# Second norms of a token mixer: row sums carried by the passes instead of statistics instructions, and rows gated in another order

## The chip, the cores and the metric

The kernel runs on one core of one Trainium2 chip. A core has engines that work beside each other, each with its own queue in a fixed order: TensorE (PE) for matrix products, VectorE (DVE) and ScalarE (ACT) for passes over the elements of a tile, GpSimd (POOL) likewise but slower, and SyncE (SP), which here issues the DMAs. They hand over by semaphores. The metric is the time of one execution on the device in microseconds (us), as the median of several runs; smaller is better.

## The reference

A block of a sequence mixer on 2048 tokens with 640 channels, fp32. The layers' modulations `sa, ca, ga, sb, cb, gb` come from `silu(c) @ w_mod`.

```python
h = layernorm(x) * (1 + ca) + sa
x = x + ga * h3(h, k, v, ...)          # short and long causal convolutions, gated by h
h = layernorm(x) * (1 + cb) + sb       # h is then normalized once more inside B:
x = x + gb * B(h)                      # B: w2 . gelu(w1 . layernorm(h) + b1) + b2, over the tokens
```

What counts here is the middle: the x that leaves the first half is normalized over its 640 channels (first norm), scaled by 1 + cb and shifted by sb, normalized again (second norm), and then multiplied by w1, a product over the tokens.

## The kernel before, in words

The 2048 tokens lie as 16 tiles ("rows" j = 0 to 15) of 128 partitions by 640 channels, XR(j), rows 0 to 7 in one buffer (`xa`) and 8 to 15 in another (`xb`). The first half (lines 500 to 628) computes the long convolution as matrix products, in five chunks of 128 channels. At the end of a chunk, i1(half) (L266) leaves the convolution's result for eight rows in PSUM, gate (L293) multiplies it by A1 and adds it to x, both for eight rows at once, and spill (L300) writes x to DRAM by SP. Chunk 4 is the last one. Its second half is gated in the next stage.

The norm stage (lines 631 to 712) follows. Every engine's order is the order of the source: nothing is rescheduled. Its helpers are:

- mod_row (L353): PE spreads a row of the modulations over the partitions, ACT copies it: row 4 is CB = 1 + cb, row 3 is SB = sb, row 5 is GB.
- x1_stats (L642): on DVE, a statistics instruction for the last 128 channels of a row and one that aggregates those of the five chunks: mean and variance of the first norm.
- rstd (L307) and rstd_pool (L320): one over the root of the variance, by ACT's root, DVE's reciprocal and a step of refinement, on DVE or on POOL, where it is a chain of small instructions ("links"). rstd_pool also makes the negated mean times that.
- norm1 (L647): ACT writes the normalized row into a temporary `tmp`, of which there are six.
- mod_stats (L651): DVE multiplies by CB, adds SB, takes two statistics of 320 channels and aggregates them.
- norm2 (L661): ACT normalizes the temporary in place and writes its upper half, rounded to fp32r, as H[j][0].
- rests (L670): DVE subtracts; the low half goes to H[j][1].
- products (L674): PE multiplies rows 2 pr and 2 pr + 1 by the first four of 14 blocks of w1. A row and a block are six products (upper by upper, upper by low, low by upper, for two halves of 320 channels, L423 in mm), so a row feeds 24, and the four blocks' results stay in the four PSUM places.

The pairs of rows pass this as a pipeline, pr = 0 to 7. After it PE runs blocks 4 to 13, then the second matrix w2. load_w(i) (L389) issues a block's load, split_w(i) (L403) splits it into upper and low halves on ACT and DVE.

psum() (L69) gives out three PSUM places in turn, and four once the norm stage has begun. The line L59 is that of the helper TT, so all tensor_tensor instructions have it.

Of the kernel before, what the change touches and what calls it, by code (L numbers as in the profile page):

```python
# [49 lines left out]
def mixer_kernel(ctx: ExitStack, tc: tile.TileContext, q, k, v, shift_k, ssm_k, ssm_D, w1, b1, w2, b2, c,  # L50
# [8 lines left out]
    TT = lambda eng, o, a, b, op: eng.tensor_tensor(o, a, b, op=op)  # L59
# [7 lines left out]
    ring = [3]  # L67

    def psum():  # L69

        uid[0] += 1
        return psp.tile([128, 1024], F32, name=f"pst_{uid[0]}", tag=f"pst{uid[0] % ring[0]}", bufs=1)

    def dram(t, offset, ap):
        return bass.AP(tensor=t.tensor, offset=t.offset + offset, ap=ap)
# [6 lines left out]
    T_g, T_rows, T_t, sm = mem("g", 1280), mem("rows", 640), mem("t", 1280), mem("sm", 704)  # L82
# [23 lines left out]

    def small(n):
        so[0] += n
        assert so[0] <= 704
        return sm[:, so[0] - n:so[0]]  # L110

    cols = small(36)
# [3 lines left out]
    rs1, nm1, rs2, nm2, tm = small(16), small(16), small(16), small(16), small(16)  # L116
    ones = small(64)
    msk = small(1)
    epsc = small(1)
    B1C, B2C = cols[:, 0:14], cols[:, 14:30]  # L120

# [144 lines left out]
    def i1(half):  # L266

        ps = psum()
        for jj in range(8):
            for ri in range(2):  # L270
                for e in range(2):
                    p = slice(64 * e, 64 * e + 64)
                    for b in range(2):
                        n2 = 16 * b + 8 * half + jj
                        pe.matmul(ps[64 * b:64 * b + 64, 512 * e + 64 * jj:512 * e + 64 * jj + 64],  # L275
                                  V1[p, ri, n2], T2[p, :, 32 * ri + n2], start=ri == 0, stop=ri == 1)
        return ps
# [12 lines left out]
            ac, po = [lambda j=j: both(j) for j in range(16)], []  # L290
        return ac, po

    def gate(c, ps, half, eng=pool):  # L293
        a = A1[:, 8 * half:8 * half + 8]
        av = a.rearrange("p j (m e) -> p e j m", e=2)
        TT(dve, av, ps.rearrange("p (e j m) -> p e j m", e=2, j=8), av, ALU.mult)
        x = XH[half][:, :, DC * c:DC * c + DC]
        TT(eng, x, x, a, ALU.add)

    def spill(c):  # L300
        for half in range(2):
# [51 lines left out]
    def mod_row(i, t):  # L353

        ps, j = psum().rearrange("p (h m) -> p h m", h=2), i % 3
        for h in range(2):
            pe.matmul(ps[:, h, 0:320], ones[32 * j:32 * j + 1, 0:1].to_broadcast([1, 128]),
                      t[32 * j:32 * j + 1, 320 * h:320 * h + 320], start=True, stop=True)
        ps = ps[:, :, 0:320]
        two = lambda t: t.rearrange("p (h m) -> p h m", h=2)  # L360
        if i == 0:
            act.activation(two(G0), ps, AF.Copy)
        elif i == 1:
            act.activation(two(G1), ps, AF.Copy, bias=1.0)
        elif i == 2:
            TT(dve, two(G0), ps, two(G0), ALU.mult)
            TT(dve, two(G1), ps, two(G1), ALU.mult)
        elif i == 3:
            act.activation(two(SB), ps, AF.Copy)
        elif i == 4:  # L370
            act.activation(two(CB), ps, AF.Copy, bias=1.0)
        else:
            act.activation(two(GB), ps, AF.Copy)
# [15 lines left out]
    def load_w(i, t=X):  # L389
        if i >= NF + NW:  # L390
            return
        if i < NF:
            t = j16(t)
            for b in range(2):
                sync.dma_start(t[64 * b:64 * b + 64],
                               dram(w1, 16 * b * F + fo(i), [[32 * F, 64], [F, 16], [1, 128]]))
            raw[i] = (t, [slice(0, 8), slice(8, 16)])
        else:
            t = f14(t)
            load_w2(t, i - NF, 0, 14)  # L400
            raw[i] = (t, [slice(0, 7), slice(7, 14)])
# [98 lines left out]
    for c in range(NC):  # L500
# [91 lines left out]
        if cn is None:  # L592
            for kk in range(3, 5):
                mod_part(tap, kk, pl[kk])
            split_w(3, mem("y", 4096, "wb3"))
            load_w(4)
            mod_sum(tap, T_t[:, 0:640])
        if cn is not None:
            if c:
# [1 line left out]
            if c + 2 < NC:  # L601
                load_ks(c + 2)
        for half in range(2):
            ps = i1(half)
# [33 lines left out]
    ring[0] = 4  # L638
    uid[0] = 3
    acc = []  # L640

    def x1_stats(js):  # L642
        for j in js:
            x1s(NC - 1, j)()
            dve.bn_aggr(mv[:, j, :], bst[:, j])

    def norm1(pr):  # L647
        for j in (2 * pr, 2 * pr + 1):
            act.activation(tmp[j % 6], XR(j), AF.Identity, scale=rs1[:, j:j + 1], bias=nm1[:, j:j + 1])

    def mod_stats(js):  # L651

        for j in js:
            t = tmp[j % 6]
            TT(dve, t, t, CB, ALU.mult)
            TT(dve, t, t, SB, ALU.add)
            for h in range(2):
                dve.bn_stats(bst[:, j, h, :], t[:, 320 * h:320 * h + 320])
            dve.bn_aggr(mv[:, j, :], bst[:, j, 0:2, :])

    def norm2(pr):  # L661
        for j in (2 * pr, 2 * pr + 1):
            t = tmp[j % 6]
# [4 lines left out]
            act.activation(H[j][0].bitcast(F32R), t, AF.Copy)  # L668

    def rests(js):  # L670
        for j in js:
            TT(dve, H[j][1].bitcast(F32R), tmp[j % 6], H[j][0], ALU.subtract)

    def products(pr):  # L674
        if not acc:
            acc.extend(psum().rearrange("p (h m) -> p h m", h=2) for _ in range(4))
        js = [(f_, j) for j in (2 * pr, 2 * pr + 1) for f_ in range(4)]
# [3 lines left out]
    x1_stats(range(2))  # L681
    rstd(rs1, nm1, 0, 2)
    norm1(0)
    gate(NC - 1, ps, 1)
    spill(NC - 1)
    x1_stats(range(2, 8))
    rstd_pool(rs1, nm1, 2, 6, lambda: mod_stats([0]))
    mod_stats([1])
    norm1(1)
    rstd(rs2, nm2, 0, 2)  # L690
    mod_row(5, T_t[:, 0:640])
    norm2(0)
    for pr in range(1, 8):
        mod_stats([2 * pr])
        if pr == 1:
            rests([0])
        mod_stats([2 * pr + 1])
        if pr < 7:
            rstd_pool(rs2, nm2, 2 * pr, 2, lambda: rests([2 * pr - 1 if pr == 1 else 2 * pr - 2]))
            norm1(pr + 1)  # L700
            if pr == 1:
                x1_stats(range(8, 16))
                rstd_pool(rs1, nm1, 8, 8)
            else:
                rests([2 * pr - 1])
        else:
            rests((12, 13))
            rstd(rs2, nm2, 14, 2)
        norm2(pr)
        products(pr - 1)  # L710
    rests((14, 15))
    products(7)


# [11 lines left out]
    def u_evac(f, ps):  # L726
# [3 lines left out]
        for h in range(2):  # L730
# [8 lines left out]

    m_p = mem("p", 2048, "m_p")  # L740
    TU = [[(H[j][n][:, 0:320], H[j][n][:, 320:640]) for j in js for n in range(2)]
          for js in ((0, 1), (2, 3), (4, 5), (9, 10), (11, 12), (13, 14))]
    RB = thirds(m_p, 3, 1088)

    def t_ops(i):
# [237 lines left out]
```

## Time and profile before

| what | value |
|---|---|
| median of 3 runs | 759.33 us (758.6 to 759.56) |
| the profiled execution's own time | 755.42 us |
| its span in the profile | 753.6 us |
| granted TensorE clock, mean | 0.964 |
| busy: PE, DVE, ACT, POOL | 651.3, 507.3, 291.7, 162.7 us |

Times inside the trace count from the start of the span. A row of the view in order of time says when a group of instructions began, how long it took in all, its engine, its line, its operation, tiles and shape, how many there were, and in brackets how long the engine had been idle and who ended that. A row of the view of groups says busy time, the mean of one in ns, and the idle time before. A row of the stretches has busy time and number for PE, PE's weight loads, DVE, ACT and POOL, then the granted clock, the DMA share and GB/s. The page's digits are busy tenths of 40 equal slices.

### The profile page before, as it was taken

The numbers are of one execution on the slowest core, as the hardware profiler recorded it, in microseconds if no ns is written. First come the engines' busy times: TensorE is split into PE (matmuls) and PEld (weight loads), VectorE is DVE, ScalarE is ACT, GpSimd is POOL, SyncE is SP. The second block draws the span as 40 slices with busy tenths as digits, with TensorE's granted clock in tenths as the row PEclk, the third lists the DMA queues.
The fourth block names the chain that finished last, engine by engine and source line by source line (L and its number), as shares of the span: only waits on it lengthen the run. The fifth ranks groups of instructions, "written<-read, shape, count | busy, mean of one in ns | idle before, by whom it ended". The sixth has DMA issues, their size and how long they took to land.

```text
span 753.6 us, 20751 instructions
## 1 busy us (share of the span) xinstructions
PE 651.3 (86%) x9117; PEld 625.8 (83%) x9117; DVE 507.3 (67%) x889; ACT 291.7 (39%) x424; POOL 162.7 (22%) x167
## 2 busy tenths in 40 slices
PE   0598947698998988971799999999999989999997
PEld 0498737697898978850799999999999988999997
DVE  4667659975977936958998413113178959888887
ACT  0342324444553544544476523123134312332322
POOL 2359003802904805503452000000000000000000
PEclk9999979989999999975899999999999999999999
DMA  9998886218142036574000352533443252555420
GB/s 163 256 230 246 244 219 139 67 38 167 39 80 59 3 60 216 151 139 100 1 1 1 59 110 57 100 69 57 105 131 103 85 166 97 151 168 167 119 77 35
DMA packets 172425, 84.26 MB, mean 112 GB/s; under 512 B 88959, under 2 KB 164910, under 8 KB 172334
## 3 DMA queue, kind: packets, MB, share of 16 engines
q1 hardware_dynamic: 168110, 81.88, 44.2%
q10 hardware_dynamic: 4224, 1.05, 0.9%
q8 instruction: 71, 1.16, 0.7%
q14 instruction: 20, 0.16, 0.1%
HBM read 72.43 MB, written 10.49 MB: 110 GB/s over the span
## 4 chain that ended last, share of the span: by engine, by line
PE 53%; DVE 22%; POOL 7%; issue 5%; DMA 5%; ACT 5%; SPq 2%; ACTq 0%; DVEq 0%; POOLq 0%
PE pst L423 25%; PE pst L214 8%; PE pst L924 7%; POOL y L59 5%; PE pst L230 5%; DVE m_w L59 4%; PE pst L259 3%; PE pst L275 3%; DVE m_x L59 3%; ACT m_w L837 2%; DVE sm L525 2%; PE pst L849 2%; DVE tap L59 1%; DMA p<-in_B_w_dram 1%; DVE m_v L59 1%
## 5 line engine op out<-in xcount | busy, mean ns | idle before, releaser
L230 PE MATMUL pst<-z,w 128*64 128x64 f32 x2560 | 96.1, 240 | 7.6 <-ACT z L216 6.1
L230 PEld LDWEIGHTS pst<-z,w 128*64 128x64 f32 x2560 | 94.6, 141 | 9.5 <-ACT z L216 7.3
L59 POOL TENSOR_TENSOR y<-p 128x256 f32<-128x256 f32 x72 | 91.1, 1311 | 31.2 <-DVE p L59 30.9
L423 PE MATMUL pst<-r_z,wb 128*128 128x320 f32 x504 | 82.1, 319 | 16.1 <-ACT r_z L668 10.9
L423 PEld LDWEIGHTS pst<-r_z,wb 128*128 128x128 f32 x504 | 78.3, 196 | 18.0 <-ACT r_z L668 12.1
L216 ACT ACTIVATE z<-pst 128x1024 f32<-128x1024 f32 x40 | 45.7, 1142 | 68.8 <-PE pst L214 48.0
L59 DVE TENSOR_TENSOR p<-pst,kt 128x512 f32<-128x512 f32 x80 | 52.9, 690 | 27.0 <-ACT kt L234 18.6
L214 PEld LDWEIGHTS pst<-v,x 128*64 128x64 f32 x640 | 46.5, 222 | 6.6 <-POOL y L59 3.0
L214 PE MATMUL pst<-v,x 128*64 128x128 f32 x640 | 48.1, 317 | 4.1 <-DVE x L59 4.1
L423 PE MATMUL pst<-h_x,wb 128*128 128x320 f32 x336 | 51.1, 309 | 0.0
L423 PEld LDWEIGHTS pst<-h_x,wb 128*128 128x128 f32 x336 | 49.7, 188 | 0.0
L234 ACT ACTIVATE kt<-pst 128x512 f32<-128x512 f32 x40 | 25.2, 629 | 55.2 <-PE pst L230 27.2
L849 PE MATMUL pst<-r_z,m_w 128*128 128x320 f32 x222 | 43.1, 313 | 3.0 <-DVE m_w L59 2.5
L259 PEld LDWEIGHTS pst<-v,y 32*128 32x128 f32 x1280 | 39.5, 193 | 6.1 <-issue 3.4
L59 DVE TENSOR_TENSOR wb<-x,wb 128x1024 fp32r<-128x1024 f32 (+1 forms) x32 | 36.8, 1189 | 10.8 <-ACT wb L412 10.7
L259 PE MATMUL pst<-v,y 32*128 32x64 f32 x1280 | 41.2, 278 | 3.3 <-issue 2.0
L729 ACT ACTIVATE pst<-pst,sm 128x640 f32<-128x640 f32 x14 | 10.7, 766 | 86.0 <-PE pst L423 86.0
L214 PE MATMUL pst<-v,p 128*64 128x128 f32 x640 | 36.9, 274 | 3.6 <-ACT p L161 2.2
L275 PEld LDWEIGHTS pst<-z,v 64*64 64x64 f32 x1280 | 21.4, 140 | 21.7 <-issue 16.8
L849 PEld LDWEIGHTS pst<-r_z,m_w 128*128 128x128 f32 x222 | 34.8, 188 | 5.0 <-DVE m_w L59 4.1
L423 PE MATMUL pst<-h_a,wb 128*128 128x320 f32 x252 | 38.8, 309 | 0.0
L423 PE MATMUL pst<-r_v,wb 128*128 128x320 f32 x252 | 38.8, 309 | 0.0
(209 smaller groups left out, 1258.3 us busy)
## 6 DMA issues: line engine op xcount, KB each, us to landing
x<-in_B_w_dram SPq DMA_DIRECT2D x24, 512.0 KB
m_v<-in_B_w_dram SPq DMA_DIRECT2D x15, 384.0 KB
x<-in_B_w_dram SPq DMA_DIRECT2D x14, 384.0 KB
in<-in_A_k_dram SPq DMA_DIRECT2D x40, 128.0 KB
aux<-in_A_ssm_k_dram SPq DMA_DIRECT2D x10, 512.0 KB
m_x<-xs SPq DMA_DIRECT2D x28, 160.0 KB
out_dram<-m_x SPq DMA_DIRECT2D x28, 160.0 KB
w<-in_const_w_dram SPq DMA_DIRECT2D x2, 2048.0 KB
```

The lines of the kernel that those rows point to most:

```text
L59: TT = lambda eng, o, a, b, op: eng.tensor_tensor(o, a, b, op=op)
L214: pe.matmul(ps[64 * ri:64 * ri + 64, o:o + 128], lhs, F1[:, 128 * ri:128 * ri + 128], start=True, stop=True)
L216: evac = lambda: act.activation(Z[:, side, t].rearrange("p a k e -> p e a k"), ps.rearrange("p (e a k) -> p e a k", a=8, e=2), AF.Copy)
L230: pe.matmul(ps[64 * h:64 * h + 64, o:o + 64], W2[k1 // 32][:, 2 * (k1 % 32) + ri], rhs, start=True, stop=True)
L234: act.activation(kt.rearrange("p (m i) -> p m i", i=32), pv[:, :, 1], AF.Copy)
L259: pe.matmul(pp[qd // 2][:, o:o + 64], Y[p, ri, i:i + 2].rearrange("p i k -> p (i k)"), V2[p, 64 * ri:64 * ri + 64], start=ri == 0, stop=ri ...
L275: pe.matmul(ps[64 * b:64 * b + 64, 512 * e + 64 * jj:512 * e + 64 * jj + 64], V1[p, ri, n2], T2[p, :, 32 * ri + n2], start=ri == 0, stop=r ...
L423: pe.matmul(ps[0:m, h, 0:320], w_.bitcast(F32R), r_[:, 320 * h:320 * h + 320].bitcast(F32R), start=first and i == 0, stop=last and i == 2)
L525: dve.bn_stats(bst[:, j, h, :], XR(j, 320 * h, 320))
L837: act.activation(W[n][0].bitcast(F32R), a(w_), AF.Copy)
L849: pe.matmul(bank[n], w[:, i].bitcast(F32R), r.bitcast(F32R), start=i == 0 and k == 0, stop=i == 6 and k == 2)
L924: pe.matmul(acc[s][:, h, 0:320], w[:, f_].bitcast(F32R), u[r + h].bitcast(F32R), start=f_ == 0 and k == 0, stop=f_ == NF - 1 and k == 2)
```

## The change

The second norm no longer takes statistics. scaled(pr) multiplies a row by CB with scalar_tensor_tensor, which also gives the row's sum. centred(pr) makes minus the mean out of it and the sum of SB (which ACT's copy of SB now carries, `msb`) and adds that and SB in one pass. ACT squares the centred row, carrying the sum of squares (the squares themselves go to the place of the low half and are not used), and takes the root. root(pr) refines on POOL. halves(pr) scales and rounds on ACT in one pass; rests(pr) makes the low half with scalar_tensor_tensor out of the unscaled row. So a row has three DVE passes and three ACT passes of 640, where it had three passes, two statistics and an aggregation on DVE and three passes on ACT.

Around it, rows 0 to 3 of the last chunk's first half are gated before the stage, rows 4 to 7 inside it; the gate of the second half (rows 8 to 15) moves behind the root of rows 4 to 7; the first products begin with three blocks, as the fourth PSUM place still holds that half; the order of pairs is written anew; there are eight temporaries, in X, P and `g`; row 5 of the modulations goes up; the spill is split by halves; and load_w(4) goes behind the products of pair 5. The new line numbers: scaled L659, centred L664 and L667, the squares L672 and their root L673, root L679 to L685, halves L688, rests L692, norm1 L653, x1_stats L502 and L649, the negated mean of SB L372.

```diff
-    def gate(c, ps, half, eng=pool):
-        a = A1[:, 8 * half:8 * half + 8]
+    def gate(c, ps, half, eng=pool, j0=0, j1=8):
+        a = A1[:, 8 * half + j0:8 * half + j1]
...
         elif i == 3:
-            act.activation(two(SB), ps, AF.Copy)
+            act.activation(two(SB), ps, AF.Copy, accum_out=msb)
+            dve.tensor_scalar(msb, msb, -1 / D, None, op0=ALU.mult)
...
-            load_w(4)
             mod_sum(tap, T_t[:, 0:640])
...
-                gate(c, ps, 0, dve)
+                gate(c, ps, 0, dve, 0, 4)
...
-    mod_row(4, T_t[:, 0:640])
-    mod_row(3, T_t[:, 0:640])
+    s0, s1, s2 = ((uid[0] + i) % 3 for i in (-1, 0, 1))
+    mod_row(4, T_t[:, 0:640], s2)
+    mod_row(3, T_t[:, 0:640], 3)
+    mod_row(5, T_t[:, 0:640], s2)
...
-    H = (unit(r_z[:, 0:4096], 3) + unit(mem("aux", 4096, "h_a"), 3) + unit(r_v, 3)
+    H = (unit(r_z[:, 0:4096], 3) + unit(r_v, 3) + unit(mem("aux", 4096, "h_a"), 3)
          + unit(r_z[:, 3840:7680], 3))
-    tmp = piece(mem("p", 2048, "t_p"), 2) + piece(mem("g", 1280, "t_g"), 2) + piece(T_t, 2)
+    tmp = piece(X, 3) + piece(mem("p", 2048, "t_p"), 3) + piece(mem("g", 1280, "t_g"), 2)
...
-    def mod_stats(js):
-        for j in js:
-            t = tmp[j % 6]
-            TT(dve, t, t, CB, ALU.mult)
-            TT(dve, t, t, SB, ALU.add)
-            for h in range(2):
-                dve.bn_stats(bst[:, j, h, :], t[:, 320 * h:320 * h + 320])
-            dve.bn_aggr(mv[:, j, :], bst[:, j, 0:2, :])
...
+    def scaled(pr):
         for j in (2 * pr, 2 * pr + 1):
+            t = tmp[j % 8]
+            dve.scalar_tensor_tensor(t, t, 1.0, CB, op0=ALU.mult, op1=ALU.mult, accum_out=su[:, j:j + 1])
+
+    def centred(pr):
+        n = su[:, 2 * pr:2 * pr + 2]
+        dve.tensor_scalar(n, n, -1 / D, msb, op0=ALU.mult, op1=ALU.add)
+        for j in (2 * pr, 2 * pr + 1):
+            t = tmp[j % 8]
+            dve.scalar_tensor_tensor(t, t, su[:, j:j + 1], SB, op0=ALU.add, op1=ALU.add)
+        for j in (2 * pr, 2 * pr + 1):
...
-            act.activation(t, t, AF.Identity, scale=rs2[:, j:j + 1], bias=nm2[:, j:j + 1])
-            act.activation(H[j][0].bitcast(F32R), t, AF.Copy)
+            act.activation(H[j][1].bitcast(F32R), tmp[j % 8], AF.Square, accum_out=sq[:, j:j + 1])
+        act.activation(tm[:, 2 * pr:2 * pr + 2], sq[:, 2 * pr:2 * pr + 2], AF.Sqrt, scale=1 / D, bias=epsc)
+
+    def root(pr):
+        c2 = slice(2 * pr, 2 * pr + 2)
+        v_, r_, t_ = sq[:, c2], rs2[:, c2], tm[:, c2]
+        pool.tensor_scalar(v_, v_, 1 / D, EPS, op0=ALU.mult, op1=ALU.add)
+        dve.reciprocal(r_, t_)
+        TT(pool, t_, r_, r_, ALU.mult)
+        TT(pool, t_, t_, v_, ALU.mult)
+        pool.tensor_scalar(t_, t_, -0.5, 1.5, op0=ALU.mult, op1=ALU.add)
+        TT(pool, r_, r_, t_, ALU.mult)
+
+    def halves(pr):
+        for j in (2 * pr, 2 * pr + 1):
+            act.activation(H[j][0].bitcast(F32R), tmp[j % 8], AF.Identity, scale=rs2[:, j:j + 1])
...
+    x1_stats(range(4))
+    rstd(rs1, nm1, 0, 4)
     norm1(0)
...
     norm1(1)
+    gate(NC - 1, ps0, 0, dve, 4)
+    spill(NC - 1, (0,))
+    scaled(0)
+    centred(0)
+    scaled(1)
+    root(0)
+    centred(1)
+    halves(0)
+    x1_stats(range(4, 8))
+    root(1)
+    rests(0)
+    products(0, range(3))
+    rstd_pool(rs1, nm1, 4, 4, lambda: gate(NC - 1, ps, 1))
+    products(0, [3])
+    halves(1)
+    spill(NC - 1, (1,))
+    norm1(2)
+    rests(1)
+    products(1)
+    scaled(2)
+    centred(2)
+    norm1(3)
+    x1_stats(range(8, 16))
+    for pr in range(2, 8):
...
+            scaled(pr + 1)
+        root(pr)
+        if pr == 2:
+            rstd_pool(rs1, nm1, 8, 8)
+        if pr < 6:
+            norm1(pr + 2)
+        if pr < 7:
+            centred(pr + 1)
+        halves(pr)
+        if pr > 2:
+            rests(pr - 1)
+            products(pr - 1)
+        if pr == 6:
+            load_w(4)
+    rests(7)
     products(7)
```

The loop over the pairs before had, per pair, mod_stats of both rows, rstd_pool of the second norm, norm1 of the next pair, rests, norm2, and products of the pair before.

More of the change, by code (lines that the diff above doesn't have):

```diff
@@ L66, in mixer_kernel, with psum @@
     xs = drp.tile([S, D], F32, name="xs")
-    ring = [3]
-    def psum():
+    ring = [0, 1, 2]
+    def psum(slot=None):
         uid[0] += 1
-        return psp.tile([128, 1024], F32, name=f"pst_{uid[0]}", tag=f"pst{uid[0] % ring[0]}", bufs=1)
+        slot = ring[uid[0] % len(ring)] if slot is None else slot
+        return psp.tile([128, 1024], F32, name=f"pst_{uid[0]}", tag=f"pst{slot}", bufs=1)
     def dram(t, offset, ap):
@@ L118, in mixer_kernel @@
     msk = small(1)
+    su, sq, msb = small(16), small(16), small(1)
     epsc = small(1)
@@ L291, in a1_ops, with spill @@
         return ac, po
-    def gate(c, ps, half, eng=pool):
-        a = A1[:, 8 * half:8 * half + 8]
+    def gate(c, ps, half, eng=pool, j0=0, j1=8):
+        a = A1[:, 8 * half + j0:8 * half + j1]
         av = a.rearrange("p j (m e) -> p e j m", e=2)
-        TT(dve, av, ps.rearrange("p (e j m) -> p e j m", e=2, j=8), av, ALU.mult)
-        x = XH[half][:, :, DC * c:DC * c + DC]
+        TT(dve, av, ps.rearrange("p (e j m) -> p e j m", e=2, j=8)[:, :, j0:j1], av, ALU.mult)
+        x = XH[half][:, j0:j1, DC * c:DC * c + DC]
         TT(eng, x, x, a, ALU.add)
-    def spill(c):
-        for half in range(2):
+    def spill(c, halves=range(2)):
+        for half in halves:
             for b in range(2):
@@ L603, in mixer_kernel @@
         for half in range(2):
-            ps = i1(half)
+            ps0, ps = ps, i1(half)
             if c:
@@ L666, in norm2 @@
             H[j] = H[j][:, 0:640], H[j][:, 640:1280]
-            act.activation(t, t, AF.Identity, scale=rs2[:, j:j + 1], bias=nm2[:, j:j + 1])
[L668 to L677, printed above, removed]
+            act.activation(H[j][1].bitcast(F32R), tmp[j % 8], AF.Square, accum_out=sq[:, j:j + 1])
@@ new lines, in halves, with rests, products @@
+    def halves(pr):
+        for j in (2 * pr, 2 * pr + 1):
+            act.activation(H[j][0].bitcast(F32R), tmp[j % 8], AF.Identity, scale=rs2[:, j:j + 1])
+    def rests(pr):
+        for j in (2 * pr, 2 * pr + 1):
+            dve.scalar_tensor_tensor(H[j][1].bitcast(F32R), tmp[j % 8], rs2[:, j:j + 1], H[j][0], op0=ALU.mult,
+                                     op1=ALU.subtract)
+    def products(pr, fs=range(4)):
+        for f_ in fs:
+            if f_ == len(acc):
+                acc.append(psum().rearrange("p (h m) -> p h m", h=2))
+        js = [(f_, j) for j in (2 * pr, 2 * pr + 1) for f_ in fs]
@@ L741, in mixer_kernel @@
     TU = [[(H[j][n][:, 0:320], H[j][n][:, 320:640]) for j in js for n in range(2)]
-          for js in ((0, 1), (2, 3), (4, 5), (9, 10), (11, 12), (13, 14))]
+          for js in ((0, 1), (2, 6), (7, 8), (9, 10), (11, 12), (13, 14))]
     RB = thirds(m_p, 3, 1088)
```

44 lines of the change are left out of this document (7 added, 37 removed).

## The prediction

> **What bounds the kernel now.** I read the page first, then the stretches of 10 us around the hole in TensorE's row, then the order of time of PE there, then the chain that ended last.
>
> ```profile
> PE   0598947698998988971799999999999989999997
> DVE  4667659975977936958998413113178959888887
> ```
> ```profile
> 340.00:350.00 10.00, 2.50 (x4) 1.16 (x4) 8.79 (x28) 2.71 (x5) 5.02 (x5) 0.57 0.74 164
> 350.00:360.00 10.00, 3.08 (x10) 2.68 (x11) 8.03 (x21) 5.62 (x8) 0.90 (x4) 0.50 0.00 1
> 360.00:370.00 10.00, 7.19 (x42) 6.66 (x40) 9.18 (x28) 5.33 (x8) 4.46 (x14) 0.91 0.01 2
> 370.00:380.00 10.00, 8.08 (x44) 8.08 (x45) 9.72 (x21) 6.68 (x10) 5.20 (x10) 0.83 0.00 1
> 380.00:390.00 10.00, 10.00 (x70) 10.00 (x69) 9.62 (x19) 6.14 (x9) 5.28 (x12) 1.00 0.01 2
> ```
>
> Each digit is 18.84 us. PE is starved in the norm stage, the 1 at 339 to 358 us and the 7 behind it, while DVE is 8 to 9.7 of 10 busy (third group of numbers); the granted clock, behind POOL's number, is at about half while PE starves. After 380 PE is full. So only what feeds PE before that moment counts.
>
> ```profile
> 355.97 0.90 PE L423 MATMUL pst<-r_z,wb 128*128 128x320 f32 x2 [10.43 <-ACT r_z L668]
> 357.83 8.80 PE L423 MATMUL pst<-r_z,wb 128*128 128x320 f32 x46 [0.95 <-DVE r_z L59]
> 367.13 0.56 PE L423 MATMUL pst<-r_z,wb 128*128 128x320 f32 x2 [0.51 <-ACT r_z L668]
> 371.92 5.03 PE L423 MATMUL pst<-r_z,wb 128*128 128x320 f32 x22 [4.23 <-DVE r_z L59]
> 376.79 10.74 PE L423 MATMUL pst<-h_a,wb 128*128 128x320 f32 x72
> 387.37 10.74 PE L423 MATMUL pst<-r_v,wb 128*128 128x320 f32 x72
> ...
> 422.61 2.80 PE L423 MATMUL pst<-r_z,wb 128*128 128x320 f32 x18
> ```
> ```profile
> 371.18 0.70 DVE r_z L59
> 371.88 0.04 issue
> 371.92 88.10 PE pst L423 x588
> ```
>
> A row of the token matrix feeds 24 products; 72 go from 376.79 to 387.37, 0.147 us each, 3.53 a row, 7.06 a pair. The first 50 are done early, then PE waits 4.23 us for the low half of row 2. From 371.92 on the chain is PE without a hole, and the fifth block starts at 422.61, after 334 more products, 50.69 us.
>
> ```profile
> 379.54 1.68 DVE L59 TENSOR_TENSOR t_g<-t_g,kt 128x640 f32<-128x640 f32 x2
> 386.57 1.68 DVE L59 TENSOR_TENSOR t<-t,kt 128x640 f32<-128x640 f32 x2
> ```
>
> The same step of DVE returns after 7.03 us: DVE needs a pair's 7.06 too, so it keeps up. A cheaper pair on DVE brings nothing from 371.92 on; **the gain can only come from an earlier last restart of PE**.
>
> **The yardstick.** Pair 0 and 1 give 96 products to the changed kernel before it needs row 4: its order on DVE puts rests(2) (L692) behind the sums of rows 8 and 9 (scaled(4)) and their centring. If PE runs dry there and restarts at T with the 99th product, it has 48 fewer to do than before at 371.92, so the fifth block starts at T + 50.69 - 48 x 0.147 = T + 43.63. That is 422.61 at **T = 379.0**: later is a loss, microsecond by microsecond. (The half clock after a restart is in the 50.69; the 22 products from 371.92 to 376.79 lost 4.87 - 3.23 = 1.6 us to it, and the 46 from 357.83 lost 2.0, so a restart varies by 0.4 in the rows shown.)
>
> **Prices.**
>
> ```profile
> L59 DVE TENSOR_TENSOR t_g<-t_g,kt 128x640 f32<-128x640 f32 x12 | 9.8, 814 | 0.2
> L858 DVE SCALAR_TENSOR_TENSOR m_x<-pst,sm,m_x 128x320 f32<-128x320 f32 x17 | 9.3, 546 | 0.0
> L858 DVE SCALAR_TENSOR_TENSOR m_x<-m_x,sm 128x320 f32<-128x320 f32 x6 | 3.3, 546 | 0.0
> L288 DVE SCALAR_TENSOR_TENSOR aux<-xa,sm,g 128x128 f32<-128x128 f32 x8 | 2.8, 347 | 0.0
> L59 DVE TENSOR_TENSOR sm<-sm 128x2 f32<-128x2 f32 x9 | 1.5, 162 | 0.3
> ```
>
> The new DVE passes are scalar_tensor_tensor of 640: from 128 (0.347) to 320 (0.546) an element costs 1.04 ns, so 0.546 + 0.33 = 0.87, starting 0.79 apart; low end the plain pass (0.81). The sum that a pass carries is shown nowhere: it can't shorten the pass, and at most adds a short instruction of its own, 0.162. I take 0.10, nearer to that row. On paper a row's DVE work falls from 7.03 / 2 to about 2.6.
>
> [...]
>
> ```profile
> 341.95 1.73 ACT L649 ACTIVATE t_p<-xa,sm 128x640 f32<-128x640 f32 x2 [1.28 <-DVE sm L318]
> 361.21 0.27 DVE L499 BATCH_NORM_STATS2 sm<-xb 128x6 f32<-128x128 f32 x1
> ...
> 364.87 0.29 DVE L645 BATCH_NORM_AGGREGATE sm<-sm 128x2 f32<-128x30 f32 x1
> ```
> ```profile
> L325 ACT ACTIVATE sm<-sm 128x2 f32<-128x2 f32 x6 | 1.7, 287 | 5.6 <-DVE sm L659 5.6
> ```
>
> An ACT pass is 0.91, two are 1.73. A square with its sum gets 0.19 more, between nothing and a small ACT instruction (0.287). Statistics of eight rows are 361.21 to 365.17, 0.49 a row.
>
> ```profile
> 361.59 0.47 POOL L59 TENSOR_TENSOR sm<-sm 128x2 f32<-128x2 f32 x2
> 372.72 1.60 POOL L59 TENSOR_TENSOR sm<-sm 128x2 f32<-128x2 f32 x2
> 343.14 2.35 POOL L59 TENSOR_TENSOR xb<-xb,aux 128x1024 f32<-128x1024 f32 x1 [30.42 <-DVE aux L59]
> 112.50 2.36 POOL L59 TENSOR_TENSOR xa<-xa,aux 128x1024 f32<-128x1024 f32 x1
> ```
> ```profile
> 112.60 2.40 DVE L289 SCALAR_TENSOR_TENSOR aux<-aux,sm,g 128x128 f32<-128x128 f32 x1
> ```
>
> POOL's small links take 0.2 each beside DVE statistics (361.59) and 0.8 beside two-input passes (372.72). The other way round, a pass of the new kind, 0.35 by its group, took 2.40 beside POOL's gate of 2.36. So the new passes and POOL shut each other out, and the change takes away just those statistics during which POOL was quick.
>
> **The walk**, part by part, in the trace's time (each duration from the rows above; links between engines 0.03 to 0.06).
>
> ```profile
> 336.20 1.22 DVE L59 TENSOR_TENSOR aux<-pst,aux 128x1024 f32<-128x1024 f32 x1
> 337.45 1.23 DVE L59 TENSOR_TENSOR xa<-xa,aux 128x1024 f32<-128x1024 f32 x1
> 339.28 0.70 ACT L371 ACTIVATE kt<-pst 128x640 f32<-128x640 f32 x1 [3.84 <-PE pst L357]
> 339.88 0.70 ACT L369 ACTIVATE kt<-pst 128x640 f32<-128x640 f32 x1
> ```
>
> 1. Gating four rows halves both DVE steps: done at 337.6 instead of 338.7. But the next DVE instruction (L372, the negated mean of SB) waits for SB with its sum on ACT, 339.88 + 0.70 + 0.19: 340.8. Queued behind it: the statistics of rows 0 to 3 and all that follows. The early gating is lost, 2 us with it.
> 2. Four rows' statistics, 1.95, and the root (eight small links of 0.16 to 0.2 with their hand-overs, 1.6): 344.4. Gating rows 4 to 7, 1.4, lies beside the first ACT pass. Sums and centring of rows 0 and 1: 349.4; sums of 2 and 3: 351.2, beside ACT's squares and root; centring them 353.1; statistics of rows 4 to 7: 355.0. Rows 0 and 1 are scaled on ACT 354.4 to 356.1, their low halves on DVE 355.3 to 357.0.
> 3. PE starts in earnest at **356.2 instead of 357.83**: a gain of 1.6, no more.
> 4. The gate of the second half now comes here: DVE 356.9 to 358.2, POOL 358.2 to 360.6 (before: 343.14, beside statistics). POOL's gate and DVE's low half of row 2 come ready within 0.1 us of each other. I let POOL win; then the root of rows 4 to 7 queues behind it on POOL, and DVE's low halves of rows 2 and 3 until 362.2, still early enough for PE. Five POOL links: 363.1. ACT's first pass of rows 4 and 5 from there, their sums, centring: 367.8.
> 5. Then DVE does the statistics of rows 8 to 15, 3.9: 371.7. PE's 96 products, at half clock first, are out at 371.5. Sums of rows 6 and 7: 373.4; only now the reciprocal for rows 4 and 5, four POOL links to 375.8, and seven more for rows 8 to 15: 377.6. ACT has its pass of rows 8 and 9 queued ahead of scaling rows 4 and 5 and waits for those seven. Pass 377.7, sums to 380.4, squares of 6 and 7 to 381.1, their root, reciprocal 381.6, centring of 8 and 9 383.3, low half of row 4: **384.2**.
>
> The same walk through the order before gives 372.3 where the trace has 371.92; I take that 0.4 off: T = 383.8, **4.8 us late**; with 0.2 for the restart, whose phase was the better one before, 5.0. After it a pair costs DVE 5.3 and ACT about 5.8, under PE's 7.06, so no further hole. What is removed per row (two statistics of 320, an aggregation, a plain pass) lies under PE's products from there on.
>
> ```profile
> 317.49 11.01 DMA p<-in_B_w_dram
> ```
>
> What costs nothing: the third mod row, moved up (PE idles there; its ACT copy, 0.7, ends before the first root needs ACT, and would delay it by that much otherwise); the new places for H and U (same tiles and sizes); the split spill (SP is idle; it is due only at row 12). The fifth block's first weight load moves behind the low half of row 11, at about 400, and is due when PE frees its block near 421. The longest wait for such a load is 11.01, so 10 us of cover are left; without them PE would wait for the excess. SP has nothing behind it that is due sooner.
>
> The profiled execution took 755.42 (span 753.6, 1.8 around it); 5.0 more is 760.4. The median of the runs is 759.33, 3.9 above that; with the same 5.0, **764.3**.
>
> **Rivals.**
> - *Cheaper chain, still slower.* Ten sums and four squares with theirs lie on the chain. Free of charge they give T 382.2, +3.2; POOL not held by these passes +2.5; plain passes' 0.80 and free sums together +1.7. For it: no row prices a sum. Against: L289's 2.40. About 762. Chance 0.17.
> - *Dearer chain.* Sums at 0.17 and 0.30 give +6.3; POOL's gate losing its 0.1 us race to a low half at 358 adds 1.0; a restart with a whole slow window more adds up to 1.5. About 767. Chance 0.17.
> - [...] Chance 0.04.
> - *Faster.* 21 DVE passes of 640 lie on the chain to T. If they ran at two elements a step, 0.33 less each, 7.0 comes off: T 376.8, -2, 757. It decides from T below 377.5, that is 0.30 off each pass. For it nothing but the lack of a row of 640; against it each row of 128, 320 and 640 shown. Chance 0.05.
> - *No change*: PE isn't dry at 371, because the chain of step 5 overlaps more than I see; T 378 to 380, 759 to 760. Chance 0.09.
>
> **How the numbers follow.** Forecast 0.48, dearer 0.21, cheaper 0.17 (all slower, less 0.01 that falls under the bound); even 0.09; faster 0.05. About 0.2% (1.5 us) is what the measurement can tell from no change: faster 0.05, same 0.10, slower 0.85. The range leaves out the faster case and the all-halved one: from 760.0 (light chain, +1) to 768.5 (+9).
>
> **What would show it.** Right: DVE idle some 3 us at 338 to 341 behind L372; PE's first products near 356, 96 of them, then a hole of about 12 us that ends with DVE r_v L692; DVE waiting on ACT and ACT on POOL at 373 to 383; the fifth block near 427. Wrong: no hole, or one that ends before 379; passes of 640 far from 0.87; POOL's links at 0.2 throughout.

## The result, and the profile after

| what | before | after |
|---|---|---|
| median beside each other, 14 runs each | 758.76 us | 761.03 us |
| ratio to before | 1 | 1.0045, 95% interval 1.0024 to 1.0065 |
| the profiled execution's own time, its span | 755.42, 753.6 us | 760.55, 758.8 us |
| granted TensorE clock, mean | 0.964 | 0.957 |

0.0045 of 759 us is 3.4 us more (the two medians are only 2.3 apart); on the 759.33 of the table before, 762.7, against 764.3 forecast.

The page's digits of after (PE and DVE), and its stretches of 10 us around the hole:

```profile
PE   0597948698998989972679999999999989999997
DVE  5657669974977936949793322212268958888887
```
```profile
350.00:360.00 10.00, 3.83 (x13) 3.43 (x14) 9.54 (x23) 6.97 (x15) 5.69 (x13) 0.50 0.11 30
360.00:370.00 10.00, 10.00 (x70) 10.00 (x69) 7.92 (x16) 4.03 (x9) 3.69 (x7) 1.00 0.22 54
370.00:380.00 10.00, 2.46 (x17) 2.19 (x15) 6.54 (x22) 3.53 (x6) 3.37 (x11) 0.85 0.00 1
380.00:390.00 10.00, 6.47 (x31) 6.08 (x32) 8.99 (x18) 9.94 (x20) 5.14 (x10) 0.64 0.00 0
```

PE is full already at 360 to 370, where it had 7.19 before, and then falls to 2.46 of 10, while DVE, ACT and POOL are busy 6.5, 3.5 and 3.4 of 10: none of them is the bound there, they wait for each other. In the page's digits PE's 179 (339 to 396 us) became 267. DVE's 84 behind that became 33: the work saved on DVE is seen, but where PE shows a 9 anyway.

PE in order of time, first of before (the start of the stage, whose other rows the prediction shows), then of after:

```profile
337.85 1.35 PE L357 MATMUL pst<-t,sm 1*128 1x320 f32 x8
```
```profile
339.29 1.35 PE L359 MATMUL pst<-t,sm 1*128 1x320 f32 x8
...
356.15 12.78 PE L426 MATMUL pst<-r_z,wb 128*128 128x320 f32 x72 [13.33 <-ACT r_z L688]
368.77 3.69 PE L426 MATMUL pst<-r_v,wb 128*128 128x320 f32 x24
382.31 0.90 PE L426 MATMUL pst<-r_v,wb 128*128 128x320 f32 x2 [9.85 <-ACT r_v L688]
384.43 8.30 PE L426 MATMUL pst<-r_v,wb 128*128 128x320 f32 x46 [1.22 <-DVE r_v L692]
392.57 10.74 PE L426 MATMUL pst<-h_a,wb 128*128 128x320 f32 x72
...
427.81 2.80 PE L426 MATMUL pst<-r_z,wb 128*128 128x320 f32 x18
```

96 products (72 + 24), a hole, two products, and the last restart at 384.43 with the 99th. I measure the **stage** from PE's first product for a modulation row to its first product of the fifth block: 422.61 - 337.85 = 84.76 before, 427.81 - 339.29 = 88.52 after, 3.76 more. The other 1.44 of the 5.2 between the spans stands ahead of the stage. Of that nothing is read: among the runs below that have the same code ahead of the stage as after, it starts anywhere from 336.43 (e5) to 340.50 (e2). The rest behind the fifth block is 331.0 in both.

The chain that ended last, from the sums of rows 6 and 7 on, names the links of the hole:

```profile
372.32 1.43 DVE t_g L659 x4
...
374.19 0.82 POOL sm L59
...
375.08 0.72 POOL sm L683
...
378.04 1.73 ACT x L653 x2
379.77 1.45 ACT h_a L672 x4
...
382.70 0.88 DVE x L667
383.58 0.81 DVE r_v L692
...
384.43 184.34 PE pst L426 x1246
```

Row 4's low half (L692) waits for the centring of rows 8 and 9 (L667), for ACT's squares of rows 6 and 7 and its pass of rows 8 and 9 (L653), and that for POOL's root of rows 8 to 15, which stands behind the one of rows 4 and 5. From 384.43 on the chain is PE alone.

### The profile page after: what moved, and what is told of

Its sections match the earlier page's. It is cut to its first block, busy times and chain, and to the rows that moved or that the text cites. A ratio compares the mean times of both kernels' runs of the same rounds, so it can differ in the third digit from the quotient of the medians.

```text
span 758.8 us, 20735 instructions
## 1 busy us (share of the span) xinstructions
PE 651.9 (86%) x9117; PEld 626.5 (83%) x9117; DVE 493.6 (65%) x856; ACT 291.3 (38%) x441; POOL 160.0 (21%) x165
## 4 chain that ended last, share of the span: by engine, by line
PE 52%; DVE 19%; POOL 8%; DMA 6%; issue 5%; ACT 4%; SPq 4%; ACTq 0%; DVEq 0%; POOLq 0%
PE pst L426 24%; PE pst L216 8%; PE pst L959 7%; POOL y L59 5%; PE pst L232 5%; DVE m_w L59 4%; PE pst L261 3%; PE pst L277 3%; DVE m_x L59 3%; DVE sm L528 2%; DMA in<-in_A_k_dram 2%; PE pst L884 2%; DMA p<-in_B_w_dram 2%; ACT m_w L872 1%; DVE m_x L893 1%
## 5 line engine op out<-in xcount | busy, mean ns | idle before, releaser
L426 PE MATMUL pst<-r_z,wb 128*128 128x320 f32 x504 | 79.5, 313 | 13.3 <-ACT r_z L688 13.3
L426 PEld LDWEIGHTS pst<-r_z,wb 128*128 128x128 f32 x504 | 76.3, 192 | 14.3 <-ACT r_z L688 13.8
L426 PE MATMUL pst<-r_v,wb 128*128 128x320 f32 x252 | 40.9, 318 | 11.1 <-ACT r_v L688 9.9
L216 PEld LDWEIGHTS pst<-v,x 128*64 128x64 f32 x640 | 43.7, 221 | 6.3 <-POOL y L59 2.7
L216 PE MATMUL pst<-v,x 128*64 128x128 f32 x640 | 45.4, 304 | 3.8 <-DVE x L59 3.8
L426 PEld LDWEIGHTS pst<-r_v,wb 128*128 128x128 f32 x252 | 38.9, 195 | 11.7 <-ACT r_v L688 10.1
L261 PEld LDWEIGHTS pst<-v,y 32*128 32x128 f32 x1280 | 41.4, 200 | 5.7 <-issue 3.1
L261 PE MATMUL pst<-v,y 32*128 32x64 f32 x1280 | 43.2, 286 | 2.8 <-issue 1.6
L216 PE MATMUL pst<-v,p 128*64 128x128 f32 x640 | 38.8, 281 | 3.8 <-ACT p L163 2.0
L216 PEld LDWEIGHTS pst<-v,p 128*64 128x64 f32 x640 | 36.5, 142 | 4.8 <-DVE aux L59 2.3
```

What stands on the lines that cost most here:

```text
L216: pe.matmul(ps[64 * ri:64 * ri + 64, o:o + 128], lhs, F1[:, 128 * ri:128 * ri + 128], start=True, stop=True)
L261: pe.matmul(pp[qd // 2][:, o:o + 64], Y[p, ri, i:i + 2].rearrange("p i k -> p (i k)"), V2[p, 64 * ri:64 * ri + 64], start=ri == 0, stop=ri ...
L426: pe.matmul(ps[0:m, h, 0:320], w_.bitcast(F32R), r_[:, 320 * h:320 * h + 320].bitcast(F32R), start=first and i == 0, stop=last and i == 2)
```

## The experiments

One theory, the prediction's: **the order makes the loss**, by what stands ahead of row 4 in DVE's, ACT's and POOL's queues. The rivals: one of the pieces (the wait for SB's sum, the gate on POOL, POOL's root) is the loss by itself, or **the arithmetic** is, whatever the order. "T" is PE's last restart behind a wait of 0.9 us or more, counted from the start of the stage. The last but one column is what the restart loses: the time from T to the fifth block less 0.147 us for each product left.

| run | stage | T | products left | lost after T | ratio to before (interval) or one time |
|---|---|---|---|---|---|
| before | 84.76 | 34.07 | 334 | 1.6 | 1 |
| after | 88.52 | 45.14 | 286 | 1.3 | 1.0045 (1.0024 to 1.0065) |
| e1_late_mean | 87.88 | 44.13 | 286 | 1.7 | 760.16 beside 759.12 |
| e2_pool_gate_early | 89.63 | 45.70 | 286 | 1.9 | 762.91 beside 759.12 |
| e3_root_on_dve | 91.00 | 47.17 | 286 | 1.8 | 761.97 beside 759.12 |
| e4_row4_ahead | 87.49 | 50.91 | 238 | 1.6 | 758.7 beside 759.12 |
| e5_rows4to7_first | 84.65 | 53.97 | 190 | 2.8 | 0.9966 (0.9944 to 0.9987) |
| e6_old_order | 78.41 | 19.69 | 382 | 2.6 | 0.990 (0.9873 to 0.9927) |
| e7_old_order_four_rows | 80.75 | 22.04 | 382 | 2.6 | 0.9921 (0.9894 to 0.9948) |
| e8_rows4to7_first_late_mean | 83.34 | 53.95 | 190 | 1.5 | 0.997 (0.9948 to 0.9992) |
| e9_old_order_row5_late | 76.94 | 18.24 | 382 | 2.6 | 0.9898 (0.9874 to 0.9921) |
| e10_old_order_early_mean | 78.32 | 19.61 | 382 | 2.6 | 0.9911 (0.9887 to 0.9935) |
| e11_before_again | 85.78 | 34.03 | 334 | 2.7 | 755.75, one run |

### e1_late_mean: the wait for SB's sum

```diff
-            dve.tensor_scalar(msb, msb, -1 / D, None, op0=ALU.mult)
...
     scaled(0)
+    dve.tensor_scalar(msb, msb, -1 / D, None, op0=ALU.mult)
     centred(0)
```

> The changed kernel with one instruction moved: the negated mean of SB is made just before the first centring instead of right behind the copy of SB. Measure: the stage, from the first mod-row product on PE to the first product of the fifth block; it is 84.76 us in the trace before (337.85 to 422.61) and 88.52 in the changed kernel (339.29 to 427.81). Theory (the order of the stage makes the hole; this wait is a small part of it, since the first POOL gate and ACT's copies come in its place): DVE's 3.56 us of idle time go, the first product comes 1 us earlier, the hole ends 1 us earlier, stage 87.4. Rival (this early wait is the main loss, as everything on DVE stands behind it): stage 85.0 or less. Second rival (the new passes and their contention with POOL are the loss): no change beyond 0.5.

Measured 87.88, T 1.0 earlier, the hole nearly as long (9.47 us and 1.22 behind two products, where it was 9.85 and 1.22). In after, DVE waited at L372:

```profile
342.15 0.15 DVE L372 TENSOR_SCALAR sm<-sm 128x1 f32<-128x1 f32 x1 [3.56 <-ACT kt L371]
```

Without that, DVE's variance is ready at 341.4, but the root on ACT stands behind ACT's copies (the rows of ACT first, then that of DVE):

```profile
342.13 0.20 ACT L371 ACTIVATION_READ_ACCUMULATOR kt<-pst 128x1 f32 x1
343.08 0.70 ACT L375 ACTIVATE rows<-pst 128x640 f32<-128x640 f32 x1 [0.74 <-PE pst L359]
343.68 0.20 ACT L314 ACTIVATE sm<-sm 128x4 f32<-128x4 f32 x1
```
```profile
343.91 0.18 DVE L315 RECIPROCAL sm<-sm 128x4 f32<-128x4 f32 x1 [2.53 <-ACT sm L314]
```

DVE now waits 2.53 us there instead of 3.56 at L372. Most of the wait removed comes back one step later: it is worth 1.0 us, and isn't the loss.

### e2_pool_gate_early: the second half's gate beside statistics

```diff
     gate(NC - 1, ps0, 0, dve, 4)
     spill(NC - 1, (0,))
+    gate(NC - 1, ps, 1)
+    spill(NC - 1, (1,))
+    x1_stats(range(4, 8))
     scaled(0)
...
-    x1_stats(range(4, 8))
...
-    rstd_pool(rs1, nm1, 4, 4, lambda: gate(NC - 1, ps, 1))
```

(The root of rows 4 to 7 goes behind the sums of rows 2 and 3, and the first pass of rows 4 and 5 ahead of root(1).)

> The changed kernel with the gate of rows 8 to 15 and the statistics of rows 4 to 7 in front of the first summing passes, as in the order before; the rest of the order is that of the changed kernel. Theory (what makes the hole is that rows 4 and 5 stand behind the statistics, root and first pass of rows 8 to 15): PE's first product comes 4 us later, the hole still ends near the same time, since the same work lies in front of row 4: stage 88.9, hole 7 us instead of 11. Rival (POOL's gate of 2.4 us in the chain is the loss): hole ends at least 2.4 us earlier, stage 86.1 or less.

Measured 89.63, and the hole is the 7 us that the theory had (5.54, two products, 1.22):

```profile
362.00 13.02 PE L426 MATMUL pst<-r_z,wb 128*128 128x320 f32 x72 [16.81 <-ACT r_z L688]
...
384.08 0.90 PE L426 MATMUL pst<-r_v,wb 128*128 128x320 f32 x2 [5.54 <-ACT r_v L688]
386.20 8.85 PE L426 MATMUL pst<-r_v,wb 128*128 128x320 f32 x46 [1.22 <-DVE r_v L692]
```

PE starts 4.6 us later in the stage than in after (362.00 - 340.50 against 356.15 - 339.29) and restarts 0.6 later. So the gate's place isn't the loss: away from the chain behind the first products, it brings the restart no sooner.

### e3_root_on_dve: no POOL links in the second norm

```diff
     def root(pr):
-        pool.tensor_scalar(v_, v_, 1 / D, EPS, op0=ALU.mult, op1=ALU.add)
+        dve.tensor_scalar(v_, v_, 1 / D, EPS, op0=ALU.mult, op1=ALU.add)
...
-        TT(pool, r_, r_, t_, ALU.mult)
+        TT(dve, r_, r_, t_, ALU.mult)
```

> The changed kernel with the second norm's refinement on DVE instead of POOL (six small instructions of 0.16 to 0.2 us per pair added to DVE, POOL's chains of 1.0 to 2.8 us gone). It tells the rival on the contention of the new passes with POOL from the order. Theory (order): stage between 88.2 and 89.5. Rival (POOL's links, held up by the two-input passes, are the loss; two such chains lie on the path): stage 86.5 or less.

Measured 91.00, dearer than either: T 2.0 later. A root's links take 1.0 us there instead of some 2.5, but they stand in the queue of the engine that has everything else to do. The root of pair 1 (L680) now comes behind the statistics of rows 4 to 7 and ahead of the low halves of pair 0:

```profile
355.79 0.16 DVE L680 RECIPROCAL sm<-sm 128x2 f32<-128x2 f32 x1
...
356.59 0.16 DVE L59 TENSOR_TENSOR sm<-sm 128x2 f32<-128x2 f32 x1
356.76 1.68 DVE L692 SCALAR_TENSOR_TENSOR r_z<-x,sm,r_z 128x640 fp32r<-128x640 f32 x2
```

So taking the links off POOL doesn't win the loss back. What POOL's slow links cost by themselves isn't told apart here, since the run adds DVE work in their place; e6, which keeps these roots on POOL and has no loss, says that they alone don't make it.

### e4_row4_ahead and e5_rows4to7_first: the order at the hole

e4 finishes pair 2 before the root of rows 8 to 15; e5 finishes pairs 2 and 3 first, with the statistics of rows 8 to 15 in two groups between them.

```diff
...
+    scaled(3)
+    root(2)
+    centred(3)
+    halves(2)
+    x1_stats(range(8, 12))
+    rests(2)
+    products(2)
+    root(3)
+    halves(3)
+    x1_stats(range(12, 16))
+    rests(3)
+    products(3)
+    rstd_pool(rs1, nm1, 8, 8)
+    norm1(4)
+    norm1(5)
+    scaled(4)
+    centred(4)
+    for pr in range(4, 8):
...
```

(The diff of e5; norm1(3) goes ahead of centred(2).)

> The changed kernel with one pair moved: scaling, low halves and products of rows 4 and 5 come right behind the centring of rows 6 and 7, ahead of the root and first pass of rows 8 to 15. Theory (order): the first hole ends near 376 in the walk's time instead of 384, a second hole of about 4 us opens at the next pair, which now waits for the same chain; stage 86.3. Rival (the passes): the hole only moves, stage 88.5 within 0.7.

> Edit: the changed kernel with another order of its steps from row 4 on, nothing else: rows 4 to 7 go through their sums, centring, halves and products before the statistics of rows 8 to 15 (taken in two groups of four between them), and the root of rows 8 to 15 on POOL comes only then. Measure of the stage: from PE's first product for a modulation row to its first product of the fifth block; before 84.76 us, changed kernel 88.52, the order with row 4 scaled ahead 87.49 (its first hole ended 6.5 us earlier, but the wait for rows 8 and 9 took most of it back). Theory (the order around rows 4 to 9 makes the hole, the new passes are cheap enough): PE gets pairs 2 and 3 without a long hole, one remains ahead of row 8; stage 82.0 to 83.5, time about 2 us under the kernel before, ratio 0.996 to 0.999. Rival (the passes of DVE and POOL's links shut each other out so much that every order runs dry for as long, as in the three orders that gave 87.5 to 89.6): stage 87 or more, ratio 1.003 or more.

e4 measured 87.49, between its two bounds:

```profile
376.96 8.36 PE L426 MATMUL pst<-r_v,wb 128*128 128x320 f32 x46 [0.36 <-DVE r_v L692]
386.92 0.56 PE L426 MATMUL pst<-h_a,wb 128*128 128x320 f32 x2 [1.60 <-ACT h_a L688]
389.27 12.08 PE L426 MATMUL pst<-h_a,wb 128*128 128x320 f32 x70 [1.80 <-DVE h_a L692]
```

The first hole ends at 38.60 in the stage instead of 45.14, 6.5 us sooner, and a second one ahead of row 6 takes nearly all of it back, since the sums and centring of rows 8 to 11 now stand ahead of the low halves of rows 6 and 7 on DVE. In e5 both are served first and the hole moves to row 8, where 190 products are left; the time falls below before, 0.9966. Its stage of 84.65 missed the 82.0 to 83.5 expected. The rows behind the last restart show what was lost there, e5 first, then e8, whose T is the same:

```profile
390.40 6.18 PE L426 MATMUL pst<-h_a,wb 128*128 128x320 f32 x22 [1.80 <-DVE h_a L692]
396.42 10.74 PE L426 MATMUL pst<-r_z,wb 128*128 128x320 f32 x72
```
```profile
393.70 4.89 PE L425 MATMUL pst<-h_a,wb 128*128 128x320 f32 x22 [1.80 <-DVE h_a L691]
398.43 10.74 PE L425 MATMUL pst<-r_z,wb 128*128 128x320 f32 x72
```

The same 22 products, 3.2 us at full pace, took 6.0 and 4.7. The granted clock was 0.68 and 0.83 in the stretch from 390 to 400 us, and 1.00 in both in the ten behind it: what was granted after the restart wasn't the same. With e8's loss, e5's stage would have been in the range.

### e8_rows4to7_first_late_mean

e1's edit on top of e5.

> Edit: as e5_rows4to7_first, and the negated mean of SB moved to just ahead of its first use, so that DVE takes the statistics of rows 0 to 3 without the wait of 3.56 us. Theory (the wait is worth what it was in the changed kernel with this one edit: stage 0.6 shorter, products in earnest 1.0 earlier, the rest eaten by the root of ACT that queues behind the copies of SB and CB): stage 0.5 to 1.2 us shorter than that of e5_rows4to7_first. Rival (with the hole gone the 3 us that DVE gains arrive whole): 2.5 us or more shorter.

The stage is 1.31 shorter, near the 1.2 expected, but by luck: all of it lies behind T, where the granted clock differed. T is 53.97 and 53.95, the ratios 0.9966 and 0.997. PE's four products for row 5, e5 first, then e8:

```profile
338.62 1.34 PE L359 MATMUL pst<-t,sm 1*128 1x320 f32 x4 [0.84 <-ACT kt L374]
```
```profile
341.94 2.28 PE L359 MATMUL pst<-t,sm 1*128 1x320 f32 x4 [0.84 <-ACT kt L373]
```

In e8 they took 0.94 longer (after's four took 1.34 at a granted clock of 1.00, before's 2.50 at 0.50), and ACT's copy of row 5 and the first root behind it came that much later. So the first products start 16.83 into the stage, as in e5 (16.86), and not at e1's 15.87. What the wait at L372 is worth in this order, this pair can't say; the 1.0 us of e1 would be some 0.001 of the time, less than the intervals.

### e6_old_order: the new arithmetic in the order before

The stage's order in this run:

```python
    x1_stats(range(2))
    rstd(rs1, nm1, 0, 2)
    norm1(0)
    gate(NC - 1, ps, 1)
    spill(NC - 1)
    x1_stats(range(2, 8))
    rstd_pool(rs1, nm1, 2, 6, lambda: scaled(0))
    dve.tensor_scalar(msb, msb, -1 / D, None, op0=ALU.mult)
    centred(0)
    norm1(1)
    root(0)
    halves(0)
    for pr in range(1, 8):
        scaled(pr)
        centred(pr)
        rests(pr - 1)
        root(pr)
        if pr < 7:
            norm1(pr + 1)
        if pr == 1:
            x1_stats(range(8, 16))
            rstd_pool(rs1, nm1, 8, 8)
        halves(pr)
        products(pr - 1)
        ...
```

(And all eight rows of the first half gated ahead of the stage.)

> Edit: the changed kernel's arithmetic (sums in the passes, squares on ACT, halves from the unscaled row, eight temporaries) in the order of the kernel before: all eight rows of the first half gated ahead of the stage, statistics and root of rows 0 and 1 alone, the second half gated on POOL beside the statistics of rows 2 to 7, and the pairs in the old pipeline; the negated mean of SB just ahead of its first use. The third modulation row, the split load and the new places for the halves stay. Theory (the loss is the new order's; the arithmetic by itself shortens the chain to the last restart): no hole longer than some 3 us after PE has started in earnest, stage 78 to 81 against 84.76 before and 88.52 changed, so 4 to 6.5 us under the kernel before, ratio 0.991 to 0.995. Rival (the arithmetic is the loss: two sums of DVE to ACT to POOL to ACT to DVE per pair make a longer chain than the statistics did, and POOL's links beside two-input passes take four times as long): stage 85 to 88, ratio 1.000 to 1.005. Second rival (the gain of the arithmetic is real but the old order can't feed PE faster because DVE's 7.03 us a pair was not what held it): stage 84 to 85, ratio 0.998 to 1.001.

Stage 78.41, ratio 0.990: faster than both kernels. The stage is inside the theory's 78 to 81, the ratio just under its 0.991 (interval 0.9873 to 0.9927). PE has no hole behind its start, and the low half of row 2, for which before's PE waits (371.18 on DVE, 33.3 in the stage), begins at 28.3:

```profile
338.94 1.35 PE L359 MATMUL pst<-t,sm 1*128 1x320 f32 x8
...
356.76 0.90 PE L425 MATMUL pst<-r_z,wb 128*128 128x320 f32 x2 [14.29 <-ACT r_z L687]
358.63 13.06 PE L425 MATMUL pst<-r_z,wb 128*128 128x320 f32 x70 [0.97 <-DVE r_z L691]
...
417.35 2.80 PE L425 MATMUL pst<-r_z,wb 128*128 128x320 f32 x18
```
```profile
367.25 0.88 DVE L691 SCALAR_TENSOR_TENSOR r_z<-x,sm,r_z 128x640 fp32r<-128x640 f32 x1
```

So the arithmetic (with what stayed beside it and isn't told apart: the places of row 5, of the load and of the halves, and the eight temporaries) is worth 1% or 7.6 us, and the new order gives that back and 3.4 more: 1.0045 / 0.990 = 1.0147, some 11 us.

### e7_old_order_four_rows, e10_old_order_early_mean, e9_old_order_row5_late

e7 is e6 with only four rows gated ahead of the stage, the other four behind the first root. e10 is e6 with the negated mean right behind ACT's copy of SB, as in after. e9 is e6 with

```diff
-    mod_row(5, T_t[:, 0:640], s2)
...
     norm1(0)
+    mod_row(5, T_t[:, 0:640], s2)
```

> Edit: as e6_old_order, but only rows 0 to 3 of the first half are gated ahead of the stage and rows 4 to 7 right after the root of rows 0 and 1, as the change does it. Theory: gating four rows first saves nothing, since the statistics of row 0 are not what waits; the DVE steps of rows 4 to 7 (1.4 us) come in between the root and the rest: stage 0.5 to 2 us longer than that of e6_old_order. Rival (the earlier gating is a gain once nothing on DVE waits for the sum of SB): stage 1 us or more shorter than that of e6_old_order.

> Edit: as e6_old_order, with the negated mean of SB where the change has it, right behind ACT's copy of SB, so that DVE waits for that copy ahead of the statistics of rows 0 and 1. Theory (the wait lies under ACT's queue: DVE would be released at about 341.8, its two rows of statistics end at 342.9, ACT is free for the root at 343.1): stage within 0.7 us of 78.41. Rival (the wait of some 2 us is a loss of that size by itself, as the prediction's first step had it): stage 79.9 or more.

> Edit: as e6_old_order (stage 78.41 us, ratio 0.990), with the third modulation row (row 5, needed only at the very end) moved from ahead of the stage to behind ACT's first passes of rows 0 and 1. In e6_old_order the root of rows 0 and 1 on ACT waited for that row's copy (0.70, and 0.74 of idle time ahead of it) and began at 343.11 where DVE's variance was ready at 340.9. Theory (the place of row 5 costs 1.4 us there, as ACT's queue is what holds the first root): first products 1.4 us earlier, stage 76.7 to 77.7, ratio 0.987 to 0.989. Rival (PE gets its first row earlier but then waits for row 2 or 4 by as much, since the statistics of rows 8 to 15 and DVE's passes of pair 1 stand where they stood): stage 78.0 to 78.8, ratio 0.989 to 0.991, and a hole of about 1 us behind the first 48 products.

e7: the stage is 2.34 longer, a little over what was expected; 1.3 is the gating now behind the root, and 1.0 is PE's four products for row 5, which took 2.37 instead of 1.34 in that execution and held the root on ACT. The ratios' intervals overlap, so the size is open; a gain it isn't. e10: 78.32 against 78.41. The wait at L372 lies under ACT's queue, as the theory had it. e9: 76.94, products in earnest 1.45 earlier, at the cost of a hole of 0.32:

```profile
344.81 0.20 ACT L314 ACTIVATE sm<-sm 128x2 f32<-128x2 f32 x1
...
347.93 0.68 ACT L375 ACTIVATE rows<-pst 128x640 f32<-128x640 f32 x1
```

The root now follows ACT's second copy at once, and row 5's copy (L375) has moved behind the passes. Its ratio, 0.9898, misses the 0.987 to 0.989 expected and can't be told from 0.990: the gain is seen in the stage alone.

### e11_before_again

Not edited.

> The kernel before, not edited, profiled once more: how well does the measure of the stage (84.76 us in the first profile) repeat? Theory: within 1 us, so that differences of 2 us and more between the orders are theirs. Rival: it wanders by 2 us or more with the phase of the granted clock, and only the ratios of times count.

85.78 against 84.76, 1.02 apart, just over the theory's 1 us. The rows:

```profile
371.26 6.10 PE L423 MATMUL pst<-r_z,wb 128*128 128x320 f32 x22 [3.97 <-DVE r_z L59]
377.20 10.74 PE L423 MATMUL pst<-h_a,wb 128*128 128x320 f32 x72
```

T is 371.26 - 337.23 = 34.03, 0.04 from the first profile; the whole difference is the restart (2.7 lost instead of 1.6). So T repeats far better than the stage does here, and differences of about 1 us between stages are read from T, with one look at row 5's four products, which moved it by 1.0 in e7 and 0.9 in e8.

## Why the prediction was right, point by point

**The mechanism** was right: 96 products, a hole of 11 us (9.85 and 1.22; 12 forecast) that ends with DVE r_v L692, then the rest without a hole. The forecast was 5.0 us, measured were 3.8 in the stage and 3.4 by the ratio; the walk's T was 383.8, and 384.43 less the 1.44 by which that stage starts later is 383.0. The 0.8 there and 0.4 behind T (43.38 to the fifth block instead of 43.83) make the difference to 3.8.

**The term that was mis-sized** is the price of sums and squares, the cheaper rival's point, and the 762.7 lie nearer to that rival's 762 than to 764.3. On DVE in after:

```profile
372.92 0.82 DVE L659 SCALAR_TENSOR_TENSOR t_g<-t_g,kt 128x640 f32<-128x640 f32 x1
373.67 0.08 DVE L659 DVE_READ_ACCUMULATOR t_g<-t_g,kt 128x1 f32 x1
...
374.06 1.68 DVE L667 SCALAR_TENSOR_TENSOR t_g<-t_g,sm,kt 128x640 f32<-128x640 f32 x2
```

A summing pass starts the next instruction after 0.75; I had 0.79 + 0.10 = 0.89. The chain that ended last passes eight of them, not the ten that I counted (the sums of rows 8 and 9 lie beside ACT's squares): 1.1 us. The read of the sum is an instruction of its own, 0.08, that hides under the pass behind it. L667, which adds a value read from a tile, took 0.88, where 0.87 was forecast for both. ACT's squares took 0.72 to 0.74 (0.91 taken) with 0.19 for the sum, as taken; those of rows 6 and 7 took 1.45 on the chain, 1.7 in the walk. Before its 0.4 were taken off, the walk had 384.2, 1.2 later than the trace's 383.0; sums and squares make that up.

The 0.04 that the chances add to the dearer chain's 0.17, and the range's all-halved case, stand for passes dearer by far. No run shows that term: with two fp32 SBUF sources and a sum the passes took 0.82 in after, where the plain product took 0.814 before.

**Step 1** (the wait at L372 costs the early gating, "2 us with it") saw the wait, released at 340.7 on before's time (340.8 forecast), and was wrong on its worth: 1.0 us in e1, nothing between e6 and e10 (e5 and e8 don't say). It was counted against a DVE without the wait, and ACT's queue ahead of the first root was forgotten.

**Step 3**: PE started 3.1 us earlier in the stage than before (16.86 against 19.98), not 1.6. It changed nothing, as T doesn't come from there.

**Step 4** happened as told:

```profile
359.04 2.39 POOL L59 TENSOR_TENSOR xb<-xb,aux 128x1024 f32<-128x1024 f32 x1
```
```profile
359.32 2.78 DVE L692 SCALAR_TENSOR_TENSOR r_z<-x,sm,r_z 128x640 fp32r<-128x640 f32 x1 [0.29 <-ACT r_z L688]
```

POOL won the race by 0.28 us; that it would was only chosen in the prediction, so this part is luck. The low half of row 2 took 2.78 beside POOL's gate, where that of row 3 behind it took 0.87, and ended 0.7 behind the gate. In e2, where the gate stands beside statistics, T came 0.6 later: without this collision nothing was gained.

**Step 5** is the loss: POOL's root for rows 8 to 15 ahead of ACT's pass, that ahead of scaling row 4. e4 and e5 showed it by taking it apart. e6 shows that, with this arithmetic, it is the order.

**"Costs nothing"**: the third modulation row is right for this order (DVE's variance comes after its copy) and 1.45 us of the stage wrong in the old one (e9). The moved load landed in time: ACT waited 2.9 us for it at 407, and PE none.

**What the prediction didn't see**: it said that a cheaper pair brings nothing from 371.92 on, which no run here contradicts, and left out what it brings before. In e6 the low half of row 2 starts 5.0 us sooner in the stage, and before's last hole is gone.

What stays open: the old arithmetic in the new order wasn't tried, so the two parts needn't add up; the order's 11 us are shared out between the place of the second half's root (e4, e5: 1.0045 to 0.9966) and the rest only roughly.

## What to carry to other kernels

A change that does two things, cheaper steps and a new order, is walked twice, the second time with the new steps in the old order; here one was worth -1% and the other more than +1%. Where a starved engine restarts, look for what stands ahead of its next input in each queue on the way: an instruction for a later row there costs its own time and everything that it waits for. And a wait that is taken away is worth only what the next one behind it leaves, so follow the released engine to its next hand-over before counting.

## What the runs showed of the hardware

- A pass with a sum cost DVE no more than the plain product did: 0.82 us in after beside 0.814 before, 0.75 from start to start, and 0.08 for the read-out, beside the next pass. On ACT the read-out took 0.18 to 0.19, and a square with its sum let the next pass start after 0.72 to 0.79.
- ACT's passes of 640 out of SBUF took, by their form, 0.72 to 0.74 for a copy or a square, 0.81 to 0.83 with a scale from a tile, 0.90 to 0.92 with scale and bias from tiles.
- The restart behind the last wait lost 1.3 to 2.8 us (table). In after, where it lost 1.3, the granted clock was 0.50 from 384.43 to 387.00 us, 0.95 in the next 3 us and 1.00 behind them. The loss isn't the same for the same work: 1.6 and 2.7 in two executions of the kernel before, whose T was the same to 0.04 us, and 2.8 and 1.5 in e5 and e8. A difference of that size in the stage of one profiled execution says nothing.
